# Inner sums in two PSUM banks in turn from the ninth turn on, in a fused attention and gated feed-forward kernel

## The chip, the core and the metric

The kernel runs on one core of one Trainium2 chip. The metric is the device time of one execution in microseconds (us). A core has TensorE (PE in the profile; its weight loads are shown apart as PEld), VectorE (DVE), ScalarE (ACT), GpSimd (POOL) and SyncE (SP), whose queue issues nearly all DMAs here. Matmuls write to PSUM, which this program uses as eight banks of 128 partitions by 512 fp32 values; a bank can be written anew only when the engines that read its last contents are done.

## The reference

Causal attention by blocks of 64, for 8 batches of 8 heads of 576 positions and 64 channels, and behind it a feed-forward layer on the 4608 tokens of 512 channels, with 2048 inner channels and a sigmoid gate:

```
scores = scale * (q @ k.T);  masked where block_i < block_j
attn = softmax(scores);      x = attn @ v, heads side by side: 4608 x 512
h = x @ w_in
out = (h * (1 / (1 + exp(-1.702 * h)))) @ w_out
```

## The kernel before

**Two streams on one PE.** The attention goes by pairs of heads: turn n (0 to 31) makes the scores of pair n and the sums of values of pair n-1, so "the ninth turn" is n = 8. The feed-forward layer ("experts" in the code) goes by 12 tiles of 384 tokens and 16 chunks of 128 inner channels, 192 chunks in all. `moe()` is a generator that yields an estimated time for every three matmuls, and the main loop advances it between the pieces of attention after a table of due times. PE's program order is the order in which this is written (`mm` and `tr` keep it); the other engines' queues are ordered by a scheduler.

**A chunk of the feed-forward layer** is: 12 matmuls of 128x384 into the inner sum `hp` (L551; x and w_in are each split into a high and a low part, and three of the four products are summed), then on ACT tanh out of `hp` (L562), on DVE g = (tanh + 1) * hp (L563), the last reader of `hp`; on ACT the high part `gh` (L571), on POOL the low part `gl` (L82 by way of `subtract`). `second()` multiplies the chunk before this one with w_out: 9 matmuls of 128x512 into three banks `acc0` to `acc2`, the last three of them with `gl`.

**A turn of attention from n = 8 on**, by the string `"3+0/2+1 - - - V - - 4 - - - L -"`: a score group of chunks 3, 0, 2 and 1 of the query positions (four banks: two heads times two packs), V (the sums of values of the pair before: bank `o`, and bank `o0` for chunk 0), a score group of chunk 4 (four banks: two heads times two halves), L (transposes of the next q and k). Between them six chunks of the feed-forward layer pass. Score banks are read by DVE (L351: mask, scale, running minimum); ACT takes the exponent (L358); the weights are normalised (L376 on POOL, L378 on DVE for chunk 4), turned on DVE in 32x32 blocks (L385, L390), and 16 DMAs on SP (L397) bring them to the layout in which the next V reads them. V's first matmul waits for all 16. ACT copies `o` and `o0` out (L451, L450).

**Banks.** Eight tags: `acc0` to `acc2`, `h` for every `hp` (L544), `w0` to `w2`, and `w3`, which serves the conversion of weights until turn 7. `bank()` deals the attention's banks: in turn 8 from `w0` to `w2`, in later turns from all four:

```
tags = ["w0", "w1", "w2"]
if not turns["experts"]:
    tags += ["acc0", "acc1", "acc2", "h"]
elif turns["n"] > 2 * HP:          # HP = 4
    tags.append("w3")
```

A PE instruction that waits for more than one engine carries one wait itself; the others stand in wait instructions of their own ahead of it in PE's queue.

## Time and profile before

| what | value |
|---|---|
| time, median of 3 runs | 1117.67 us (1117.2 to 1118.97) |
| span of the profiled execution (first to last instruction) | 1116.9 us |
| its own time | not reported; the median lies 0.8 us over the span |
| PE matmul / weight load busy | 1082.2 us (97%) / 912.9 us (82%) |
| DVE, ACT, POOL busy | 52%, 45%, 36% |
| granted TensorE clock | 0.87 and 0.83 in the first two stretches of 40 us, 0.96 in the third, 1.00 from 120 us to 1080 us |

A matmul's record is longer than the distance to the next one: a matmul of 384 columns is recorded with 0.33 us and the next starts 0.17 us later; one of 512 columns with 0.39 us, and the next starts 0.23 us later. A busy share of PE near 100% therefore hides short waits. They are seen in the distance between starts, and in the idle time of the weight loader ahead of a matmul.

### The profile page before, as it was taken

Reading aid. Unit: us, or ns where it says so; the run is one execution under the profiler, and the core shown is the slowest. Engines: PE = TensorE matmul, PEld = TensorE weight load, DVE = VectorE, ACT = ScalarE, POOL = GpSimd, SP = SyncE. Lnnn points to the kernel's source line nnn. Section 1 sums busy time; section 2 is a strip of 40 time slices with the busy share of each in tenths; the row PEclk is TensorE's granted clock in tenths of the full one; section 3 lists DMA queues with packets and bytes.
Section 4 is the critical chain, followed back from the end, with each engine's and each line's share of the span. In section 5 each row is a group of like instructions: output and inputs, shape, how many; then the busy total and the mean of one; then the engine's idle time right before and its main releaser. Section 6 shows DMA issues by size and latency. Waiting matters only on the chain. (4 is left out here: it accounts for less than half of the span.)

```text
span 1116.9 us, 19972 instructions
## 1 busy us (share of the span) xinstructions
PE 1082.2 (97%) x6960; PEld 912.9 (82%) x6960; DVE 584.2 (52%) x1856; ACT 498.9 (45%) x1321; POOL 406.4 (36%) x509
## 2 busy tenths in 40 slices
PE   6979999999999999999999999999999999999998
PEld 4757777788888888888888888888888888899997
DVE  6786786655645645655555555645645654211210
ACT  5865775443533534534443443443444434322322
POOL 4665565332333333333333332333333333122222
PEclk8979999999999999999999999999999999999999
DMA  8634523342434433243443333344442332200000
GB/s 183 193 89 153 146 61 80 72 103 59 96 81 86 109 80 70 58 99 71 113 86 75 80 92 68 63 108 86 86 103 66 71 84 54 54 30 1 29 1 29
DMA packets 219365, 91.25 MB, mean 82 GB/s; under 512 B 197760, under 2 KB 197760, under 8 KB 219264
## 3 DMA queue, kind: packets, MB, share of 16 engines
q1 hardware_dynamic: 214528, 89.38, 34.1%
q8 instruction: 55, 0.90, 0.3%
q10 hardware_dynamic: 4736, 0.59, 0.3%
q14 instruction: 46, 0.38, 0.1%
HBM read 45.09 MB, written 9.44 MB: 49 GB/s over the span
## 5 line engine op out<-in xcount | busy, mean ns | idle before, releaser
L82 POOL TENSOR_TENSOR gl<-g,gh 128x384 fp32r<-128x384 f32 x192 | 194.5, 1013 | 555.1 <-ACT gh L571 450.4
L563 DVE SCALAR_TENSOR_TENSOR g<-g,hp 128x384 f32<-128x384 f32 x192 | 106.0, 552 | 318.6 <-ACT g L562 317.2
L99 PE MATMUL hp<-xh,wih 128*128 128x384 f32 x768 | 265.8, 346 | 2.8 <-DVE g L563 1.8
L562 ACT ACTIVATE g<-hp 128x384 f32<-128x384 f32 x192 | 94.2, 491 | 368.5 <-PE hp L99 361.0
L99 PE MATMUL hp<-xh,wil 128*128 128x384 f32 x768 | 258.7, 337 | 0.0
L99 PE MATMUL hp<-xl,wih 128*128 128x384 f32 x768 | 254.4, 338 | 0.2
L99 PE MATMUL acc<-woh,gh 128*128 128x512 f32 x576 | 233.9, 406 | 0.0
L99 PE MATMUL acc<-wol,gh 128*128 128x512 f32 x576 | 227.0, 394 | 0.0
L99 PEld LDWEIGHTS hp<-xh,wih 128*128 128x128 f32 x768 | 144.4, 188 | 30.9 <-DVE g L563 20.3
L99 PE MATMUL acc<-woh,gl 128*128 128x512 f32 x576 | 168.2, 393 | 0.3 <-POOL gl L82 0.3
L571 ACT CAST gh<-g 128x384 fp32r<-128x384 f32 x192 | 98.4, 513 | 156.8 <-DVE g L563 156.5
L99 PEld LDWEIGHTS hp<-xh,wil 128*128 128x128 f32 x768 | 144.6, 188 | 5.6
L358 ACT ACTIVATE e<-e,mx 64x64 f32<-64x64 f32 (+4 forms) x240 | 132.2, 552 | 32.2 <-DVE mx L351 32.2
L376 POOL TENSOR_TENSOR e<-e,sm 64x64 f32<-64x64 f32 (+1 forms) x192 | 113.6, 612 | 86.3 <-DVE sm L371 42.5
L99 PEld LDWEIGHTS hp<-xl,wih 128*128 128x128 f32 x768 | 144.0, 188 | 1.0 <-DVE xl L82 1.0
L99 PE MATMUL bank<-qk 64*128 64x320 f32 (+4 forms) x768 | 124.3, 432 | 16.2 <-DVE qk L297 10.4
L99 PEld LDWEIGHTS acc<-woh,gh 128*128 128x128 f32 x576 | 108.2, 188 | 34.2 <-issue 10.8
L99 PEld LDWEIGHTS acc<-woh,gl 128*128 128x128 f32 x576 | 107.6, 188 | 25.4 <-POOL gl L82 1.2
L351 DVE CUSTOM_DVE_ANT_0 e<-bank,mask 64x64 f32<-64x64 f32 (+4 forms) x240 | 89.7, 417 | 70.1 <-PE bank L99 67.0
L99 PEld LDWEIGHTS acc<-wol,gh 128*128 128x128 f32 x576 | 108.4, 188 | 16.8 <-issue 0.4
L385 DVE STREAM_TRANSPOSE turned<-e 128x384 f32<-128x384 f32 (+1 forms) x192 | 92.5, 500 | 49.5 <-POOL e L376 48.9
L99 PEld LDWEIGHTS bank<-qk 64*128 64x128 f32 x768 | 71.4, 196 | 56.4 <-issue 25.4
(50 smaller groups left out, 960.6 us busy)
## 6 DMA issues: line engine op xcount, KB each, us to landing
turned<-turned SPq DMA_DIRECT2D x192, 80.0 KB, 2.1
turned<-turned SPq DMA_DIRECT2D x96, 112.0 KB, 2.2
raw<-in_q_dram SPq DMA_DIRECT2D x128, 72.0 KB, 2.3
out_dram<-osb SPq DMA_DIRECT2D x36, 256.0 KB, 2.4
raw<-in_k_dram SPq DMA_DIRECT2D x120, 72.0 KB, 2.4
turned<-turned SPq DMA_DIRECT2D x96, 88.0 KB, 2.1
words<-in_moe_w_in_dram SPq DMA_DIRECT2D x16, 512.0 KB, 5.6
vp<-in_v_dram SPq DMA_DIRECT2D x60, 128.0 KB, 2.4
```

The lines of the kernel that those rows point to most:

```text
L82: eng.tensor_tensor(out=out, in0=in0, in1=in1, op=ALU.subtract)
L99: return tc.keep_in_program_order(nc.tensor.matmul(**kw))
L351: nc.vector.tensor_tensor_reduce(out=e[0:m, hd, lo:hi], in0=s, in1=mk, op0=ALU.add, op1=ALU.min, scale=-0.125, scalar=3e38 if lo == 0 else ...
L358: nc.scalar.activation(out=e[0:m, hd], in_=e[0:m, hd], func=AF.Exp, scale=-1.0, bias=mx[0:m, i, hd : hd + 1], accum_out=sm[0:m, i, hd : hd ...
L376: nc.gpsimd.tensor_tensor(out=x, in0=x, in1=sc.to_broadcast([m, width(i)]), op=ALU.mult)
L385: nc.vector.transpose(out=tw[:, :, SLOT[i] : SLOT[i] + i, hd].rearrange("p b j c -> p j b c"), in_=e[:, hd, 0 : i * P],)
L562: nc.scalar.activation(out=g, in_=hp[:, 0:tt], func=AF.Tanh, scale=1.702)
L563: nc.vector.scalar_tensor_tensor(out=g, in0=g, scalar=1.0, in1=hp[:, 0:tt], op0=ALU.add, op1=ALU.mult)
L571: nc.scalar.copy(out=gh, in_=g)
```

## The change

From the score group of turn 8 on ("late"), `hp` no longer has a bank of its own. Two tags, `h` and `w3`, are "now" and "spare". The first bank of every score group and V's `o0` are the spare one (`lent_bank`); all others come from `w0` to `w2`. A new `hp` swaps the two, except where the spare was lent since the last `hp`: then it takes the same bank as that one. `w3` leaves the deal of `bank()`.

```diff
-    turns = {"n": 0, "bank": 0, "experts": False}
+    turns = {"n": 0, "bank": 0, "experts": False, "late": False}
+    gate_bank = {"now": "h", "spare": "w3", "lent": False}
...
         if not turns["experts"]:
             tags += ["acc0", "acc1", "acc2", "h"]
-        elif turns["n"] > 2 * HP:
-            tags.append("w3")
...
+    def lent_bank():
+        gate_bank["lent"] = True
+        return ps.tile([P, 512], F32, tag=gate_bank["spare"], name="bank")
+
+    def next_hp():
+        if turns["late"] and not gate_bank["lent"]:
+            gate_bank["now"], gate_bank["spare"] = gate_bank["spare"], gate_bank["now"]
+        gate_bank["lent"] = False
+        return ps.tile([P, 512], F32, tag=gate_bank["now"], name="hp")
...
     def score(n, banks):
+        turns["late"] = not early(n)
...
-                ss = [bank() for _ in range(2)]
+                ss = []
+                for _ in range(2):
+                    taken += 1
+                    ss.append(lent_bank() if taken == 1 and turns["late"] else bank())
...
-        o, o0 = bank(), bank()
+        o = bank()
+        o0 = lent_bank() if turns["late"] else bank()
...
-                hp = ps.tile([P, 512], F32, tag="h", name="hp")
+                hp = next_hp()
```

PE's instructions and their order stay the same; what changes is which of them wait, and for whom. The line numbers of the changed kernel are 9 to 15 higher. In the rows below the numbers in names are those of single tiles, and `[waits ...]` names the engines (or DMA queues) whose progress the instruction waits for.

PE, turn 23, the start of the inner sum of the chunk just ahead of the score group of chunk 4 (`hp_7882`, which starts at 748.38 us in the profile before). Before:

```order
L99 MATMUL acc1_7616<-woh_410,gl_7801 128x512
L99 MATMUL acc2_7617<-woh_410,gl_7801 128x512
L99 MATMUL hp_7882<-xh_977,wih_643 128x384 [waits DVE_49]
L99 MATMUL hp_7882<-xh_977,wil_644 128x384
L99 MATMUL hp_7882<-xl_978,wih_643 128x384
```

Now:

```order
L108 MATMUL acc1_7616<-woh_410,gl_7801 128x512
L108 MATMUL acc2_7617<-woh_410,gl_7801 128x512
L108 MATMUL hp_7882<-xh_977,wih_643 128x384 [waits Activation_49]
L108 MATMUL hp_7882<-xh_977,wil_644 128x384
L108 MATMUL hp_7882<-xl_978,wih_643 128x384
```

It waited for DVE's g of the chunk just before; now it waits for ACT's copy of the `o0` that last held its bank.

PE, two chunks later, the one just ahead of the score group of chunks 3, 0, 2 and 1 (`hp_7990`, at 758.37 us). Before:

```order
L99 MATMUL acc1_7616<-woh_894,gl_7897 128x512
L99 MATMUL acc2_7617<-woh_894,gl_7897 128x512
L99 MATMUL hp_7990<-xh_977,wih_643 128x384 [waits DVE_49]
L99 MATMUL hp_7990<-xh_977,wil_644 128x384
L99 MATMUL hp_7990<-xl_978,wih_643 128x384
```

Now:

```order
L108 MATMUL acc1_7616<-woh_894,gl_7897 128x512
L108 MATMUL acc2_7617<-woh_894,gl_7897 128x512
L108 MATMUL hp_7990<-xh_977,wih_643 128x384
L108 MATMUL hp_7990<-xh_977,wil_644 128x384
L108 MATMUL hp_7990<-xl_978,wih_643 128x384
```

Its wait is gone: DVE's read of the bank (scores of chunk 4) is already implied by an earlier wait on PE. The first score matmul behind each of these two inner sums now waits for DVE (the g that last read the spare bank); two score matmuls of the group of chunk 4 lose a wait for ACT. The fifth inner sum of a turn, just ahead of V, waits for DVE and PE where it waited for DVE, and V's first matmul waits for DVE besides the DMAs and PE. PE has 198 separate wait instructions where it had 151: one more at each of these two places.

Turn 8, where `bank()` had three banks: the score group of chunk 4, on PE (its first matmul is at 201.29 us in the profile before). Before:

```order
L99 MATMUL bank_2302<-qk_1970 128x256 [waits DVE_49]
L99 MATMUL bank_2303<-qk_1970 128x256 [waits Activation_49]
L99 MATMUL bank_2306<-qk_1970 128x320 [waits Activation_49]
L99 MATMUL bank_2307<-qk_1970 128x320 [waits DVE_49]
L99 MATMUL acc0_987<-woh_1777,gl_2216 128x512 [waits Pool_49]
```

Now:

```order
L108 MATMUL bank_2302<-qk_1970 128x256 [waits Activation_49]
L108 MATMUL bank_2303<-qk_1970 128x256 [waits DVE_49]
L108 MATMUL bank_2306<-qk_1970 128x320 [waits DVE_49]
L108 MATMUL bank_2307<-qk_1970 128x320
L108 MATMUL acc0_987<-woh_1777,gl_2216 128x512 [waits Pool_49]
```

The fourth bank's matmul no longer waits for DVE's read of the group's own first bank. On DVE the scheduler shifts two rows in this turn, and no others in the program: the first g of the turn now stands between two block transposes of chunk 3 where it stood behind both, and the last block transpose of chunk 2 stands behind the split of x (`xl`) and the next g where it stood ahead of them:

```order
L399 STREAM_TRANSPOSE turned_75<-e_2189 128x2x4x32 x2
L82 TENSOR_TENSOR xl_978<-xr_72,xh_977 128x384 x4
L578 SCALAR_TENSOR_TENSOR g_2281<-g_2281,hp_2268 128x384
L404 STREAM_TRANSPOSE turned_75<-e_2189 64x2x2x32
L365 ISA e_2310,mx_2148<-bank_2302,mask_69 128x256
```

(L404 is L390 of before, L399 is L385, L578 is L563, L365 is L351.) The orders of ACT, POOL and SP are the same.

## The prediction

> **What bounds the kernel now.** I read the page first (the span, the busy shares, the costliest groups), then the waits of PE and of its weight loader from 224 to 965 us, then the timeline around the waits found there.

> ```profile
> span 1116.9 us, 19972 instructions
> PE 1082.2 (97%) x6960; PEld 912.9 (82%) x6960; DVE 584.2 (52%) x1856; ACT 498.9 (45%) x1321; POOL 406.4 (36%) x509
> L99 PE MATMUL hp<-xh,wih 128*128 128x384 f32 x768 | 265.8, 346 | 2.8 <-DVE g L563 1.8
> ```

> PE sets the end. By the page the inner sums wait for DVE's g for 1.8 us in the whole run, and there would be little to win. That column counts only idle time between records that overlap. The weight loader tells more:

> ```profile
> PEld hp L99 <- DVE g L563: 18.0, 46, 0.6
> ...
> PE bank L99 <- DMA turned<-turned: 0.7, 1, 0.7
> ```

> Between 224 and 965 us it stood idle 46 times (two in each turn) and 18.0 us in all ahead of an inner sum, for DVE's g; PE itself shows one wait in this stretch, V's last one for its DMAs. One of the 46, just ahead of the score group 3, 0, 2, 1:

> ```profile
> 788.57 0.49 ACT L562 ACTIVATE g<-hp 128x384 f32<-128x384 f32 x1 [1.60 <-PE hp L99]
> ...
> 788.91 0.67 DVE L385 STREAM_TRANSPOSE turned<-e 128x512 f32<-128x512 f32 x1
> ...
> 789.61 0.31 DVE L390 STREAM_TRANSPOSE turned<-e 64x128 f32<-64x128 f32 x1
> 789.70 0.86 PE L99 MATMUL acc<-woh,gl 128*128 128x512 f32 x3
> 789.95 0.55 DVE L563 SCALAR_TENSOR_TENSOR g<-g,hp 128x384 f32<-128x384 f32 x1
> ...
> 790.56 0.19 PEld L99 LDWEIGHTS hp<-xh,wih 128*128 128x128 f32 x1 [0.44 <-DVE g L563]
> 790.56 0.44 PE L99 MATMUL hp<-xh,wih 128*128 128x384 f32 x1
> ...
> 790.84 0.34 PE L99 MATMUL hp<-xh,wil 128*128 128x384 f32 x1
> ```

> Tanh is done at 789.06, but DVE is at its block transposes and ends g at 790.50; the next inner sum needs the same bank and starts 0.06 us later. Without the wait it would start three distances of 0.23 us behind 789.70, at 790.39: 0.17 us lost. The matmul behind it starts after 0.28 us where 0.17 is usual: 0.11 more. Together 0.28 us at an idle gap of 0.44. The turn's other kind of wait, just ahead of the score group of chunk 4:

> ```profile
> 779.84 0.86 PE L99 MATMUL acc<-woh,gl 128*128 128x512 f32 x3
> ...
> 780.57 0.19 PEld L99 LDWEIGHTS hp<-xh,wih 128*128 128x128 f32 x1 [0.32 <-DVE g L563]
> 780.58 0.44 PE L99 MATMUL hp<-xh,wih 128*128 128x384 f32 x1
> ...
> 780.86 0.34 PE L99 MATMUL hp<-xh,wil 128*128 128x384 f32 x1
> ```

> Due at 780.53: 0.05 late and 0.11 for the fresh start, 0.16 us at a gap of 0.32. In both the loss is the gap less 0.16. An inner sum whose bank was long free loses nothing, since it starts 0.69 us, three distances, behind its forerunner:

> ```profile
> 768.36 0.85 PE L99 MATMUL acc<-woh,gl 128*128 128x512 f32 x3
> 769.05 0.33 PE L99 MATMUL hp<-xh,wih 128*128 128x384 f32 x1
> ```

> **The change part by part.** No instruction of an engine comes or goes, and PE's order stays; only who waits for whom, and two rows of DVE in turn 8.

> *The 46 waits.* In a turn the six inner sums are: one ahead of chunk 4's scores (swaps banks), one behind (keeps, the spare was lent), one ahead of the other group (swaps), one behind (keeps), one ahead of V (swaps), one behind V (keeps). The two that wait are both swappers, so both go to a bank that DVE's g of the chunk just before doesn't read. Gain: 18.0 - 46 x 0.16 = 10.6 us. Ends: with nothing for the fresh start (46 x 0.11) it is 5.6; the whole 18.0 is out, as 0.16 of each gap belongs to no late start. I take 10.6, the two rows' own sum.

> *What the swapped banks wait for instead.* One was lent to chunk 4's scores, the other to `o0`, which ACT has copied out at 776.64, 3.9 us before the inner sum that takes it starts at 780.58. The spare that a score group borrows was last read by g:

> ```profile
> 757.76 0.55 DVE L563 SCALAR_TENSOR_TENSOR g<-g,hp 128x384 f32<-128x384 f32 x1
> ...
> 760.68 2.11 PE L99 MATMUL bank<-qk 64*128 64x448 f32 x16
> ...
> 776.44 0.20 ACT L450 COPY xr<-bank 128x64 f32<-128x64 f32 x1
> ```

> It is free at 758.31, and the scores start 2.37 us later (2.1 with the wait ahead of them gone). The inner sum itself, 2.1 us of PE work, is the cover of this lend and of the like one at chunk 4. Cost 0. Three `w` banks and the spare still give four different banks to each group.

> *Wait instructions.* 47 more, one ahead of the fifth inner sum and one ahead of V in most turns. V had four already; a score group had none:

> ```profile
> 760.41 0.34 PE L99 MATMUL hp<-xl,wih 128*128 128x384 f32 x1
> ...
> 770.99 0.34 PE L99 MATMUL hp<-xl,wih 128*128 128x384 f32 x1
> ...
> 771.25 0.99 PE L99 MATMUL bank<-turned,vp 128*64 128x128 f32 x16
> ```

> From the inner sum's last matmul to V: 0.26 us with four; to the scores (760.68): 0.27 us with none. A wait that is long fulfilled costs nothing there, as PE's queue runs ahead. I take 0; the upper end is the 0.11 us of a fresh start at 46 places, 5.1 us. [...]

> *V's DMAs.* Each V waits for 16 DMAs that start from chunk 4's scores by way of DVE. Between those scores and V lies one of the two waits (0.28 us), so PE now comes to V 0.28 us earlier while the DMAs keep their distance from the scores. What is spare there:

> ```profile
> turned<-turned SPq DMA_DIRECT2D x192, 80.0 KB, 2.1
> ...
> 757.41 11.40 SPq L397 DMA_DIRECT2D turned<-turned  x16
> ...
> 918.52 11.80 SPq L397 DMA_DIRECT2D turned<-turned  x16
> 932.35 0.88 PE L99 MATMUL bank<-turned,vp 128*64 128x128 f32 x14
> ...
> 941.79 2.24 PE hp L99 x12
> 960.17 2.70 DMA turned<-turned
> ...
> 963.12 2.99 PE bank L99 x60
> ```

> An issue takes 11.40/16 = 0.7 us and its DMA lands 2.1 us after the issue's start, so the last lands 1.4 us after the issues end; the last V starts 0.25 us behind its last landing (960.17 + 2.70). In turn 23: 768.81 + 1.65 = 770.46 against a start at 771.25, 0.8 us to spare. One of the two tightest turns (918.52): 930.32 + 1.65 = 931.97 against 932.35, 0.38 to spare. All above 0.28: cost 0. Only the last V waits already, and the chain of waits leaves PE at 944.03 for that stretch; the 0.28 us of the wait within it are lost.

> *Turn 8*, the start of the late part:

> ```profile
> 190.33 1.10 PE L99 MATMUL bank<-qk 64*128 64x320 f32 x6 [0.50 <-DVE mx L351]
> ...
> 194.38 0.58 DVE L385 STREAM_TRANSPOSE turned<-e 128x384 f32<-128x384 f32 x1 [0.31 <-POOL e L376]
> ...
> 204.17 0.55 DVE L563 SCALAR_TENSOR_TENSOR g<-g,hp 128x384 f32<-128x384 f32 x1
> ...
> 205.12 0.80 PE L99 MATMUL bank<-qk 64*128 64x320 f32 x2 [2.60 <-DVE mx L351]
> ...
> 206.66 0.33 PE L99 MATMUL hp<-xh,wih 128*128 128x384 f32 x1
> ...
> 210.85 10.89 SPq L397 DMA_DIRECT2D turned<-turned  x16
> 223.60 0.67 PE L99 MATMUL bank<-turned,vp 128*64 128x128 f32 x10
> ```

> With three banks a group waits for its own first bank: 0.50 and 2.60 us. Both waits go; the inner sum at 206.66 then waits for g, over at 204.72, so PE gains 1.9 us there. But V at 223.60 stands on its DMAs: 221.74 + 1.65 = 223.39, so 0.2 us are spare. DVE, busy without a break from 204.17 on, sets when they start, and gains about 0.2 us of the 0.31 idle at 194.38, into which g now falls. Net 0.4 us; ends 0 and 0.50 + 1.9 = 2.4, if the DMAs came forward as far as PE. I take 0.4, by the DMA rows.

> **The sum.** 10.6 + 0.4 - 0.3 = 10.7 us off the profiled span of 1116.9: 1106.2. The median of the runs is 0.8 us above the span, and I keep that: 1117.67 - 10.7 = 1107.0 us. The tail after 965 us has no waits for g (the distance of 768.36 to 769.05 is its rule), so nothing is won there.

> **Rivals.**
> - V's DMAs eat the share that lies between chunk 4's scores and V: 22 x 0.28 = 6.2 us back, 1113.2. For it: the last V and turn 8 stand on them already. Against: 0.38 and 0.8 to spare in the turns shown.
> - The extra wait instructions make a fresh start each: 5.1 us back, 1112.1. Against: the four ahead of V. [...]
> - Turn 8 keeps its 2.4 us: 1105.0. Against: SP issues 0.7 us apiece, from a start that DVE sets.
> - The change doesn't do what it says: a lend falls between the sums that wait and their forerunners, and they keep their bank: 1117.7. Against: the waits for DVE ahead of `hp_7882` and `hp_7990` are gone from PE's order.
> - Slower: score groups meet a spare bank whose g is late, a 2.60 us wait as at 205.12 once a turn: 23 x (2.60 - 0.46) = 49 us, 1167. It starts where g ends 2.1 us later than it does and loses more than it wins from 2.6 us on; DVE is held for about 1 us ahead of g at 788.91 to 789.92, so half of that at most.

> **How the numbers follow.** The forecast 0.74; DMAs 0.07; wait instructions 0.06; turn 8 kept 0.04; no effect 0.05; slower 0.04. Faster by over 0.2% (2.2 us, about what a measurement of this kernel can tell from no change): 0.74 + 0.07 + 0.06 + 0.04 = 0.91; within it 0.05; slower 0.04. The range takes in turn 8's case below, with 0.5 us of spread (the runs shown spread by 1.8), and the wait instructions' above, near which the low end of the 46 waits (5.6 + 0.4 - 0.3, so 1112.0) lies too: 1104.5 to 1112.2, which leaves out 0.16.

> **What would show it.** In the changed profile: the weight loader's wait of 46 times for g between 224 and 965 us gone; the second matmul of every inner sum 0.17 us behind the first; a turn shorter by 0.44 us; no wait of 0.50 and 2.60 us in turn 8, but one of about 1.5 us or more at V near 223 us for its DMAs; the last V's wait about 0.3 us longer than 0.7. Wrong would be: waits of scores or of `o0` for DVE, V waiting in most turns, or a gap ahead of the fifth inner sum of a turn.

## The result, and the profile after

| kernel | median of runs | ratio to before, 95% interval |
|---|---|---|
| before, beside it | 1117.63 us (1117.18 to 1118.97, 5 runs) | |
| changed | 1109.17 us (1107.77 to 1109.53, 5 runs) | 0.9919 [0.9907, 0.993] |
| changed, a second time (before: 1118.18 us) | 1108.38 us (1105.27 to 1110.55, 6 runs) | 0.9906 [0.9891, 0.992] |

The change wins 8.5 us; 10.7 were forecast. The time lies 2.2 us above the forecast of 1107.0 and inside its range. The page of the changed kernel, against the rows of before in the prediction:

```profile
span 1107.5 us, 19998 instructions
PE 1070.3 (97%) x6960; PEld 915.7 (83%) x6960; DVE 585.0 (53%) x1856; ACT 498.6 (45%) x1321; POOL 406.4 (37%) x509
L108 PE MATMUL hp<-xh,wih 128*128 128x384 f32 x768 | 261.1, 340 | 4.2 <-DVE g L578 3.5
```

The profiled run took 1109.41 us, so 1.9 us lie outside its span. The page would mislead again: the inner sums' idle time for g has risen, from 1.8 to 3.5 us (1.79 us of it from 82.22 us, in the part that did not change, and 1.71 new in turn 8, below), while the 46 waits that mattered are gone. In turn 23, the two places that the prediction showed at 780.58 and 790.56 us (columns: start, duration, both in us):

```profile
772.77 0.85 PE L108 MATMUL acc<-woh,gl 128*128 128x512 f32 x3
...
773.46 0.33 PE L108 MATMUL hp<-xh,wih 128*128 128x384 f32 x1
...
773.63 0.34 PE L108 MATMUL hp<-xh,wil 128*128 128x384 f32 x1
...
782.50 0.85 PE L108 MATMUL acc<-woh,gl 128*128 128x512 f32 x3
782.74 0.56 DVE L578 SCALAR_TENSOR_TENSOR g<-g,hp 128x384 f32<-128x384 f32 x1
...
783.19 0.33 PE L108 MATMUL hp<-xh,wih 128*128 128x384 f32 x1
...
783.36 0.34 PE L108 MATMUL hp<-xh,wil 128*128 128x384 f32 x1
```

Both inner sums now start 0.69 us behind their forerunner, and their second matmul 0.17 us behind the first. The second one starts at 783.19, while g of the chunk before ends only at 783.30. In turn 8 and at the two V steps that wait for DMAs:

```profile
202.60 0.44 PE L108 MATMUL hp<-xh,wih 128*128 128x384 f32 x1 [1.71 <-DVE g L578]
...
209.15 11.27 SPq L411 DMA_DIRECT2D turned<-turned  x16
...
222.23 4.64 PE L108 MATMUL bank<-turned,vp 128*64 128x128 f32 x60 [2.50 <-DMA turned<-turned]
...
953.74 2.98 PE L108 MATMUL bank<-turned,vp 128*64 128x128 f32 x60 [1.01 <-DMA turned<-turned]
```

The waits of 0.50 and 2.60 us are gone. Instead one inner sum waits 1.71 us for g, and V waits 2.50 us for its transposed copies. Then comes something that the prediction did not have: V's 60 matmuls take 4.64 us; the last V takes 2.98. The same stretch by the granted clock (columns: stretch, its length, PE's busy time and number of instructions, PE's granted clock, DMA share, GB/s):

```profile
219.00:222.00 3.00, 0.74 (x5) 1.00 0.53 122
222.00:224.00 2.00, 1.77 (x27) 0.74 0.78 126
224.00:226.00 2.00, 2.00 (x25) 0.50 0.96 257
226.00:228.00 2.00, 2.00 (x21) 0.91 0.58 221
228.00:230.00 2.00, 2.00 (x11) 1.00 0.62 139
```

**Where the time went, by stretches.** The same matmul can be found in every trace, so a kernel's gain in a stretch is read from the distance between two such matmuls. The marks are three inner sums and PE's last matmul (the table is worked out from unrounded starts). Before:

```profile
186.90 0.34 PE L99 MATMUL hp<-xh,wih 128*128 128x384 f32 x1
253.60 0.33 PE L99 MATMUL hp<-xh,wih 128*128 128x384 f32 x1
947.31 0.33 PE L99 MATMUL hp<-xh,wih 128*128 128x384 f32 x1
1112.99 0.40 PE L99 MATMUL acc<-woh,gl 128*128 128x512 f32 x1
```

After:

```profile
185.61 0.34 PE L108 MATMUL hp<-xh,wih 128*128 128x384 f32 x1
253.45 0.33 PE L108 MATMUL hp<-xh,wih 128*128 128x384 f32 x1
937.90 0.33 PE L108 MATMUL hp<-xh,wih 128*128 128x384 f32 x1
1103.61 0.39 PE L108 MATMUL acc<-woh,gl 128*128 128x512 f32 x1
```

| profile (us gained are negative) | to 186.9 | 186.9 to 253.6, turns 8 and 9 | 253.6 to 947.3 | from there to the end |
|---|---|---|---|---|
| changed | -1.28 | +1.13 | -9.25 | +0.02 |
| changed, a second time | -0.48 | +1.04 | -9.31 | +0.54 |
| turn 8 as before | -1.69 | +1.31 | -9.31 | +0.51 |
| 14 matmuls ahead of V | -0.18 | -0.66 | -9.31 | -0.63 |
| 7 matmuls ahead of V | -1.68 | -0.99 | -9.31 | +0.46 |
| V of turn 9 later | -2.08 | -3.09 | -9.31 | +0.20 |
| and the last V later | -0.34 | -3.10 | -9.30 | -1.06 |
| one swap of two | -3.12 | -0.27 | -5.51 | +0.66 |
| turn 8 alone, fourth bank from its scores on | -1.76 | -0.87 | -0.41 | -0.62 |
| the same, V of turn 9 later | -2.12 | -0.27 | -0.33 | -0.63 |

The first column is the same work in all ten (experiment 3, whose edit changes it, is left out), so its 3 us of scatter are no effect of the edits, and before's own profile is slower there than any of them. The scatter goes with the time that each trace shows at half the clock ahead of the mark: 27.3 us in before and in the three rows of -0.18 to -0.48, 23.9 us in the four of -1.28 to -1.76, 20.5 us in the two of -2.08 and -2.12, and 17.1 us in the one of -3.12. The third column is where the change pays, alike within 0.06 us in every kernel that has both swaps.

### The profile page after: what moved, and what is told of

It reads as the page before. It is cut to its first block, busy times and chain, and to the rows that moved or that the text cites. A ratio compares the mean times of both kernels' runs of the same rounds, so it can differ in the third digit from the quotient of the medians.

```text
span 1107.5 us, 19998 instructions
## 1 busy us (share of the span) xinstructions
PE 1070.3 (97%) x6960; PEld 915.7 (83%) x6960; DVE 585.0 (53%) x1856; ACT 498.6 (45%) x1321; POOL 406.4 (37%) x509
## 4 chain that ended last, share of the span: by engine, by line
PE 87%; DVE 4%; ACT 4%; issue 2%; SPq 1%; DMA 1%; POOL 1%; POOLq 0%; ACTq 0%; DVEq 0%
PE hp L108 35%; PE acc L108 35%; PE bank L108 16%; ACT turned L372 1%; PE bank L111 1%; SPq L411 1%; DVE wm L243 1%; ACT wm L228 1%; DVE turned L365 1%; DVE wm L232 1%; DVE wm L238 1%; DVE qk L306 0%; DVE xl L82 0%; DMA raw<-in_k_dram 0%; ACT turned L425 0%
## 5 line engine op out<-in xcount | busy, mean ns | idle before, releaser
L578 DVE SCALAR_TENSOR_TENSOR g<-g,hp 128x384 f32<-128x384 f32 x192 | 106.0, 552 | 312.2 <-ACT g L577 310.8
L108 PE MATMUL hp<-xh,wih 128*128 128x384 f32 x768 | 261.1, 340 | 4.2 <-DVE g L578 3.5
L108 PEld LDWEIGHTS hp<-xh,wih 128*128 128x128 f32 x768 | 144.6, 188 | 17.1 <-DVE g L578 4.4
L390 POOL TENSOR_TENSOR e<-e,sm 64x64 f32<-64x64 f32 (+1 forms) x192 | 113.6, 612 | 87.6 <-ACT e L372 45.2
L108 PEld LDWEIGHTS acc<-woh,gh 128*128 128x128 f32 x576 | 108.2, 188 | 34.2 <-issue 10.7
L108 PE MATMUL bank<-qk 64*128 64x320 f32 (+4 forms) x768 | 121.3, 428 | 13.9 <-DVE qk L306 11.3
L365 DVE CUSTOM_DVE_ANT_0 e<-bank,mask 64x64 f32<-64x64 f32 (+4 forms) x240 | 89.7, 417 | 67.5 <-PE bank L108 64.2
L108 PEld LDWEIGHTS acc<-wol,gh 128*128 128x128 f32 x576 | 108.4, 188 | 16.8 <-issue 0.4
L399 DVE STREAM_TRANSPOSE turned<-e 128x384 f32<-128x384 f32 (+1 forms) x192 | 92.5, 500 | 50.1 <-POOL e L390 48.4
```

The costliest lines, as they stand in the source:

```text
L108: return tc.keep_in_program_order(nc.tensor.matmul(**kw))
L365: nc.vector.tensor_tensor_reduce(out=e[0:m, hd, lo:hi], in0=s, in1=mk, op0=ALU.add, op1=ALU.min, scale=-0.125, scalar=3e38 if lo == 0 else ...
L390: nc.gpsimd.tensor_tensor(out=x, in0=x, in1=sc.to_broadcast([m, width(i)]), op=ALU.mult)
L399: nc.vector.transpose(out=tw[:, :, SLOT[i] : SLOT[i] + i, hd].rearrange("p b j c -> p j b c"), in_=e[:, hd, 0 : i * P],)
L578: nc.vector.scalar_tensor_tensor(out=g, in0=g, scalar=1.0, in1=hp[:, 0:tt], op0=ALU.add, op1=ALU.mult)
```

## The experiments

The time of before beside them was 1117.56 us for the first four, 1117.80 for the next four and 1118.18 for the last two.

**1. Turn 8 as before** (the change from turn 9 on).

```diff
-        turns["late"] = not early(n)
+        turns["late"] = n > 2 * HP
```

> The change from turn 9 on; turn 8 has three score banks as before. Theory A (the 46 waits are worth 10.0 us; turn 8's freed waits are not worth anything, they come back as one wait of 2.6 us at V near 222 us, in which the granted clock falls to 0.50, so that V and what follows lose 1.6 us): about 1.5 us faster than the changed kernel, 1107.6 us, with the granted clock 1.00 from 219 to 229 us. Rival B (turn 8's freed waits are a gain, and the slow V is none of their doing): slower than the changed kernel by up to 1 us, 1110 us.

Measured: 1109.06 us (1107.73 to 1110.59), ratio 0.9927 [0.9914, 0.994]: no different from the changed kernel. Its trace shows why the time could not decide: it has before's wait of 2.60 us in turn 8, but here that wait too was followed by a slow stretch. The wait in this kernel, then the two stretches behind it by the granted clock, here and in before:

```profile
203.42 0.80 PE L108 MATMUL bank<-qk 64*128 64x320 f32 x2 [2.57 <-DVE mx L365]
```

```profile
205.00:207.00 2.00, 2.00 (x9) 0.55 0.00 0
207.00:209.00 2.00, 2.00 (x8) 0.59 0.46 74
```

```profile
205.00:207.00 2.00, 1.88 (x7) 1.00 0.00 0
207.00:209.00 2.00, 2.00 (x13) 1.00 0.03 5
```

The same pause, ahead of the same matmul, is followed by half the clock in one execution and by the full clock in another. In turn 9 of experiment 1 V shows no wait and runs at full pace, as theory A expected and rival B did not:

```profile
223.64 2.99 PE L108 MATMUL bank<-turned,vp 128*64 128x128 f32 x60
```

**2. PE kept at work ahead of V** (14 matmuls into V's bank, whose sums V overwrites).

```diff
+        if n == 2 * HP:
+            for _ in range(14):
+                mm(
+                    out=o0[:, 0:TT], lhsT=weights("wih", 0)[:, 0, 0:P], rhs=xs["xh"][:, 0, 0:TT],
+                    start=True, stop=True,
+                )
```

> The changed kernel with 14 matmuls of 128x384 ahead of V in turn 9, into the bank of chunk 0's sums, whose result is overwritten: they fill 2.45 us of the wait of 2.6 us for V's DMAs and add nothing else. Theory A (the idle PE lets the clock fall): V starts at the same time, about 222.2 us, but runs at 0.05 us a matmul instead of 0.11; granted clock 1.00; 1.6 us faster than the changed kernel, 1107.5 us. Rival C (V's matmuls are slow because DMAs run at up to 376 GB/s beside them): V stays slow, 1109.2 us.

Measured: 1106.65 us (1105.47 to 1108.02), ratio 0.9907 [0.9892, 0.9921].

```profile
220.66 2.59 PE L108 MATMUL bank<-xh,wih 128*128 128x384 f32 x14
223.18 2.98 PE L108 MATMUL bank<-turned,vp 128*64 128x128 f32 x60
```

With work in the pause V runs at full pace, and the table gives 1.79 us against the changed kernel (+1.13 to -0.66) where A said 1.6. The transfers beside V are about as heavy as before (a DMA share of 0.82 from 223.2 to 226.2 us here, 0.89 from 222.2 to 226.9 us beside the slow V): the loss comes from the pause and not from them.

**3. Turn 8 alone, first attempt.** In the kernel before, the fourth bank joins the deal with turn 8:

```diff
-        elif turns["n"] > 2 * HP:
+        elif turns["n"] >= 2 * HP:
```

> The kernel before with four score banks already in turn 8 (the spare w3 joins the deal one turn earlier); the inner sums keep one bank. Theory A: the waits of 0.50 and 2.60 us in turn 8 go and come back at V near 223 us; 0 to 0.4 us faster if the clock holds, and 1.2 to 1.6 us slower if it falls: 1117.3 or 1119.0 us. Rival B: 2.4 us faster, 1115.2 us.

Measured: 1120.1 us (1118.36 to 1121.84), ratio 1.0027 [1.0016, 1.0037]. Inconclusive: the bank joined too early in the turn, while the weights' conversion still used it, and PE stood still for that:

```profile
185.08 1.06 PE L102 MATMUL bank<-ident,turned 128*64 128x128 f32 x4 [5.31 <-DVE wm L234]
```

The clock was 0.50 for the 6 us behind that.

**4. V of turn 9 one slot later**, behind one more chunk of the feed-forward layer.

```diff
+NINTH = "3+0/2+1 - - - - V - 4 - - - L -"
...
-        return {HP: START, 2 * HP: HANDOVER}.get(n, ORDER[phase(n)]).split()
+        return {HP: START, 2 * HP: HANDOVER, 2 * HP + 1: NINTH}.get(n, ORDER[phase(n)]).split()
```

> The changed kernel with V of turn 9 one slot later (about 2.5 us of feed-forward work goes ahead of it). Theory A: the wait of 2.6 us at V is filled with useful matmuls and the clock holds: 2.6 + 1.6 = 4.2 us faster than the changed kernel, 1105.0 us. Rival C (slow V by DMA traffic): only the wait goes, 2.6 us, 1106.6 us. Rival D (the later V delays what follows it in turn 9 by as much): no change, 1109.2 us.

Measured: 1104.43 us (1104.17 to 1104.61), ratio 0.9886 [0.987, 0.9902].

```profile
223.04 2.98 PE L109 MATMUL bank<-turned,vp 128*64 128x128 f32 x60
```

V waits for nothing and runs at full pace, beside a DMA share of 0.97 from 223 to 226 us, above the 0.89 of the slow V: rival C is out. Turns 8 and 9 gain 3.09 us where the change alone lost 1.13, together A's 4.2. With the swaps, turn 8's time is won as soon as V does not stand in its way.

**5. The last V later as well**: the same order of steps for the last turn.

```diff
-        return {HP: START, 2 * HP: HANDOVER, 2 * HP + 1: NINTH}.get(n, ORDER[phase(n)]).split()
+        return {HP: START, 2 * HP: HANDOVER, 2 * HP + 1: NINTH, NPAIR: NINTH}.get(n, ORDER[phase(n)]).split()
```

> The changed kernel with the V step one slot later in turn 9 (as in the run before) and, new here, in the last turn too. Theory A (the last turn's V waits on TensorE for the transposed copies, 0.7 us in the kernel before and 0.3 us more after the change, because the work ahead of it got shorter; a slot later it has the sums of a whole slot to hide behind): 0.7 to 1.0 us faster than the run with turn 9 alone, so about 1103.5 us, and no wait ahead of the last V in the trace. Rival B (the steps behind V in the last turn then come later by as much, and the end waits for them instead): no change, 1104.4 us.

Measured: 1103.82 us (1103.62 to 1104.84), ratio 0.9872 [0.9858, 0.9885], the lowest median of all. The last V in experiment 4, then here:

```profile
948.85 2.99 PE L109 MATMUL bank<-turned,vp 128*64 128x128 f32 x60 [1.18 <-DMA turned<-turned]
```

```profile
953.51 2.98 PE L109 MATMUL bank<-turned,vp 128*64 128x128 f32 x60
```

The wait is gone, and the tail is 1.26 us shorter in the trace (+0.20 against -1.06). The runs' times overlap with those of experiment 4 (1104.17 to 1104.61), so the medians' 0.6 us by themselves would prove nothing.

**6 and 7. Turn 8 alone, the bank joining at its scores; the same with V later.** To the kernel before:

```diff
-    turns = {"n": 0, "bank": 0, "experts": False}
+    turns = {"n": 0, "bank": 0, "experts": False, "four": False}
...
-        elif turns["n"] > 2 * HP:
+        elif turns["four"]:
...
     def score(n, banks):
+        turns["four"] = not early(n)
```

> The kernel before, with the fourth bank of the deal joining at turn 8's scores (at the same place where the changed kernel begins to lend), so that turn 8's part of the change is there alone and the 46 waits of the later inner sums stay. Theory A: the waits of 0.50 and 2.60 us in turn 8 go and come back as TensorE's wait for the transposed copies ahead of V near 223 us, so 0 to 0.4 us faster than the kernel before (1117.56 us); up to 1.6 us slower than that in an execution in which the granted clock halves behind that wait. Rival B (turn 8's waits are time won outright): about 2.4 us faster, 1115.2 us.

> The run above with V one slot later in turn 9. Theory A (the freed time of turn 8 was only held up by V's transposed copies): 2.5 to 4 us faster than the kernel before, so 1113.6 to 1115.1 us, with no wait at V. Together with the run of the changed kernel with the later V (1104.43 us, 13.1 us under the kernel before) it says how much the 46 waits are worth by themselves: 13.1 less this gain, 10 us by theory A. Rival B (the 46 waits are worth more than their sum, since turns that run shorter also lift the granted clock or move other waits): this run gains under 1.5 us, and 11.5 us or more are left for the 46.

Measured: 1114.87 us (1114.21 to 1115.33), ratio 0.9968 [0.9956, 0.9981], and 1115.36 us (1113.99 to 1118.14), ratio 0.9982 [0.9972, 0.9992]. By the median experiment 6 looks like rival B, and 7, which was to be the faster one, is not. The trace of 6:

```profile
202.12 0.44 PE L99 MATMUL hp<-xh,wih 128*128 128x384 f32 x1 [1.71 <-DVE g L564]
...
208.02 0.44 PE L99 MATMUL hp<-xh,wih 128*128 128x384 f32 x1 [1.45 <-DVE g L564]
...
221.15 2.99 PE L99 MATMUL bank<-turned,vp 128*64 128x128 f32 x60 [0.21 <-PE hp L99]
```

Theory A was right that most of the 3.1 us comes back, and wrong about the place: with one bank for the inner sums two of them wait for g, 3.16 us together, and then V is not early at all, so a later V has nothing to give (turns 8 and 9: -0.87 and -0.27). The sum by medians that experiment 7 was meant for (13.1 less its gain of 2.4 leaves 10.7 for the 46 waits) is therefore no measure of them. The rest of the two medians lies in stretches that this edit hardly touches: 1 us behind 253.6 (0.6 of it behind 947.3, where the last V does not wait and had waited 0.7 in before's profile), and the start. What remains of the medians is not explained by the one profile of each.

**8. One swap of two**: experiment 4, but the inner sum ahead of chunk 4's scores keeps the bank of the one before it.

```diff
...
-            gate_bank["now"], gate_bank["spare"] = gate_bank["spare"], gate_bank["now"]
+            if not gate_bank["hold"]:
+                gate_bank["now"], gate_bank["spare"] = gate_bank["spare"], gate_bank["now"]
+            gate_bank["hold"] = False
...
+        gate_bank["hold"] = turns["late"]
```

The last line stands in V, where `o` and `o0` get their banks; `hold` is False at first.

> The changed kernel with the later V of turn 9, in which the inner sum ahead of chunk 4's scores keeps the bank of the sum before it, so that one of the two waits of each turn stays and only the one ahead of score group 3, 0, 2, 1 goes. Theory A (each of the two removed waits is worth its own row, 0.28 us for the one ahead of the score group and 0.16 us for the one ahead of chunk 4's scores): 23 times 0.16 = 3.7 us slower than with both swaps (1104.43), so 1108.1 us. Rival B (the two waits cover for each other: with one gone the other grows by what was won): 23 times 0.44 = 10 us slower, 1114.5 us. Rival C (the second wait was nearly free): 1104.4 us.

Measured: 1110.8 us (1109.9 to 1111.28), ratio 0.9932 [0.9919, 0.9944]: 6.4 us slower than with both swaps, between A's 3.7 and B's 10. What the weight loader waited between 253 and 947 us in before, and in the same stretch here (250 to 939):

```profile
PEld hp L99 <- DVE g L563: 16.8, 43, 0.6
```

```profile
PEld hp L111 <- DVE g L582: 7.8, 22, 0.6
```

In that stretch the kept waits cost 9.31 - 5.51 = 3.80 us, 0.17 each: theory A's 0.16. They did not grow by what the other kind had cost: the same 22 inner sums had waited 7.8 us in before too. The other 2.8 us are turn 8's (-0.27 instead of -3.09), where an inner sum without a swap waits 1.45 us for g as in experiment 6; A had left that out.

**9. Half of the pause filled**: experiment 2 with `range(7)`.

> The changed kernel with 7 matmuls of 128x384 instead of 14 in the pause ahead of V in turn 9 (their sums are overwritten by V's own), so that about 1.2 us of TensorE's pause of 2.5 us are left. Theory A (the granted clock halves only behind pauses longer than about 1.5 us; the pauses of 1.21 and 1.27 us near 130 and 158 us were followed by a clock of 1.00 in each of the ten profiles): V's 60 matmuls take 2.98 us, as with 14, and the time is 1106 to 1107 us. Rival B (any pause at this place lets the clock fall): V takes 4.64 us, and the time is that of the changed kernel, 1109.2 us.

```profile
221.35 2.98 PE L108 MATMUL bank<-turned,vp 128*64 128x128 f32 x60 [0.81 <-issue]
```

V runs at full pace behind a pause of 0.81 us, which speaks against B, and turns 8 and 9 gain 0.99 us. The pause came out shorter than the 1.2 us that were to be left, so A's limit of 1.5 us is not tested by it. The time, 1107.87 us (1106.66 to 1108.94), ratio 0.9905 [0.9891, 0.992], is above A's 1106 to 1107 and within the scatter of the unchanged kernel beside it (1105.27 to 1110.55): the trace decides against B here, the time does not.

**10. The changed kernel again.**

> The changed kernel once more, for a second profiled execution of it. Theory A (the fall of the clock behind a pause of 1.7 to 2.6 us comes in some executions and not in others: behind the same 1.78 us pause near 83 us six profiles of ten show it): V of turn 9 waits 2.0 to 2.6 us again, and its 60 matmuls take either 4.64 or 2.98 us; the runs' times lie between 1106 and 1109.5 us. Rival B (the fall belongs to this order of work): 4.64 us again in every execution, the median within 0.3 us of 1109.2 us.

```profile
223.06 4.49 PE L108 MATMUL bank<-turned,vp 128*64 128x128 f32 x60 [2.54 <-DMA turned<-turned]
```

V was slow in both profiles of this kernel, so A's "in some executions" isn't shown for this very place (the last section says what these two had in common). The runs spread over 5.3 us around a median of 1108.38, which speaks against B's narrow time, but the start scatters too.

## Why the prediction held, and where it was off

- **The 46 waits: right, the term 6% too large.** All are gone. Of the 130 inner sums between 253.6 and 947.3 us that run without a break, the 43 that had waited are shorter by 0.216 us each on average, 9.3 us together, and the other 87 by nothing. The forecast's rule, the gap less 0.16, gives 16.8 - 43 x 0.16 = 9.9 there. The late start (0.119) and the fresh start (0.111) were sized rightly; what the rule missed is that a sum that did not wait takes 0.014 us longer from the start of its second matmul to that of its last (1.762 instead of 1.748). For all 46 that makes 10.0, not 10.6.
- **Swapped banks, lends, wait instructions at 0: right.** No score, no `o0` and no V between 224 and 953 us waits on PE. From the last matmul of a sum to the scores or V behind it stay 0.27 us on average, before and after. In the changed kernel's trace 188 of the 198 separate wait instructions are recorded with 0.051 us each, and PE's queue runs ahead of PE: the last of the five ahead of V ended 0.06 to 1.88 us before V's first matmul started, in each of the 22 turns between 224 and 953 us. The 47 added ones, an estimated 47 x 0.051 = 2.4 us of the queue's time, do not show in the 0.27 us.
- **V's DMAs: right.** PE has only one wait between 224 and 965 us, the last V's: 1.01 us where it was 0.7, the forecast 0.3 more. In other profiles of kernels with both swaps and the last V in its place that wait was 0.35 to 1.50 us, so the match to 0.3 us in this one profile is luck; what moves the wait was not settled.
- **Turn 8, 0.4 us gained: wrong.** The waits moved as forecast, on to g (1.71 us) and to V's DMAs (2.50). They gave back a little more than thought: the issues started 0.42 us earlier than the start-up's 1.28 accounts for (210.85 to 209.15), but took 11.27 us instead of 10.89, so V came forward by 223.60 - 222.23 - 1.28 = 0.1 us only. The step that failed is the silent one, that a pause costs its own length: this one was followed by half the clock, and V lost 4.64 - 2.98 = 1.66 us more. Together turn 8 cost 1.6 us (the table's 1.13, and 0.43 that two of the 46 waits won in the same stretch) instead of winning 0.4.
- **"0.8 us above the span": wrong, but the forecast of the time does not hang on it.** The median was of other runs than the span: in the runs where both are known 1.7 to 2.0 us lie outside the span (1109.41 against 1107.5 here; a later run of before with the same span of 1116.9 took 1118.85). Before's profiled execution was thus one of its slower ones. The forecast of 1107.0 is also the median of before less the gain, and this needs no such term; from the profiled span it would have been 1106.2 + 1.9 = 1108.1. The start, 1.28 us shorter in the changed kernel's profile, is chance and belongs to no term.
- **The sum, span to span:** -10.7 forecast, -9.4 measured: start -1.3, the 46 waits +0.65, turn 8 +2.0. By the medians it is -10.7 against -8.5, and the two wrong terms give -10.7 + 0.65 + 2.0 = -8.1; the other 0.4 is within the spread of the runs (1.8 us). The measured time lies inside the range, but it moved up by something for which the range made no room: its upper part stood there for wait instructions and for a fresh start worth nothing. That the half clock at V fitted into it is luck. The rivals: "DMAs eat the share" and "wait instructions" would have ended at 1113.2 and 1112.1 and would show as waits or longer distances in every turn; none is there. "Turn 8 keeps its 2.4 us" needs the later V of experiment 4. The lends that meet a late g are not seen.

## What to carry to other kernels

Where one engine's records overlap, look for lost time in the weight loader's idle gaps and in the distances between starts: 46 waits that the page put at almost nothing were worth 10 us of 1118. In turn 8 the waits removed close ahead of other bounds moved to those bounds (0.50 and 2.60 us went, 1.71 and 2.50 us came); 4.2 us (turns 8 and 9 from +1.13 to -3.09) lay in placing the next consumer, V, one slot later, about half of what the change itself had won. Compare kernels by stretches between the same instructions: a start-up that scatters by 3 us hides effects that repeat within 0.06 us elsewhere.

## What the hardware showed that was not expected

A pause of PE cost more than its length here: behind the 2.50 us ahead of V, V took 4.64 us instead of 2.98. At 83 us, in work that is the same in all kernels, PE waits 1.78 or 1.79 us for g. In before's profile the clock then halves, in that of experiment 4 it does not. For each, the row of the wait, then three stretches around it (the columns are those of the table by the granted clock above; why they are cut so is said below). Before:

```profile
83.44 0.44 PE L99 MATMUL hp<-xh,wih 128*128 128x384 f32 x1 [1.78 <-DVE g L563]
```

```profile
80.83:84.24 3.41, 1.59 (x6) 1.00 0.00 0
84.24:87.66 3.42, 3.42 (x12) 0.50 0.00 0
87.66:91.07 3.41, 3.41 (x16) 1.00 0.00 0
```

Experiment 4:

```profile
82.87 0.44 PE L109 MATMUL hp<-xh,wih 128*128 128x384 f32 x1 [1.78 <-DVE g L579]
```

```profile
78.24:81.65 3.41, 2.79 (x12) 1.00 0.00 0
81.65:85.07 3.42, 2.20 (x13) 1.00 0.00 0
85.07:88.48 3.41, 3.41 (x17) 1.00 0.00 0
```

Over the twelve profiles half the clock followed this pause 8 times; a pause of 1.58 us near 28 us 4 times in 12; pauses of 1.70 to 1.72 us in turn 8 once in 10; pauses of 2.50 to 2.60 us in turns 8 and 9 three times in 4; the one of 5.31 us too. Behind the 24 pauses of 1.21 and 1.27 us near 128 and 156 us, the three of 1.45 us in turn 8 and the four of 1.45 to 1.64 us ahead of the last V it never came.

The slow stretch behind each of these pauses lasted one window, so at half the clock an estimated 3.413 / 2 = 1.71 us of work at most was lost to it (two windows behind the 5.31 us of experiment 3). A hit (a pause followed by half the clock) cost about 1.5 us at 83 us (from that inner sum to the scores behind it 5.85 to 5.94 us instead of 4.36 to 4.39), and 1.66 and 1.51 us in the two slow V.
